# A windowed attention and a SoLU layer on one core: the last 64 rows of a^T on array halves, a late row scale, and sums of three by the reduce

## The chip, the core and the metric

The kernel runs on one core of one Trainium2 chip. Five engines work side by side, each through its own queue in order: PE (matrix products; its weight loads are shown as PEld), DVE (vector operations), ACT (activation functions with a scale and a bias), POOL (elementwise operations) and SP (which here only issues transfers). The metric is the device time of one execution in microseconds.

## The reference

Input x has 8 batches of 4160 rows of 192 numbers; each row has, for each of 8 heads, 7 weights over itself and the 6 rows before it.

```python
w = weight_gen - np.max(weight_gen, axis=-1, keepdims=True)
w = np.exp(w)
w = w / (np.sum(w, axis=-1, keepdims=True) + 1e-09)
...
out = np.einsum('bshk,bskhg->bshg', w, x_unf)        # 7 taps, 8 heads of 24
...
h = x @ w_in                                         # 192 -> 1024
e = np.exp(h - np.max(h, axis=-1, keepdims=True))
sm = e / (np.sum(e, axis=-1, keepdims=True) + 1e-09)
solu = h * sm
mu = np.mean(solu, axis=-1, keepdims=True)
var = np.mean((solu - mu) ** 2, axis=-1, keepdims=True)
ln = (solu - mu) / np.sqrt(var + 1e-06) * g_ln
return (ln @ w_out).astype(np.float32)               # 1024 -> 192
```

The result has 33280 rows of 192. The 1024-wide weights come as 64-bit floats and are turned into 32-bit ones on the chip.

## The kernel before

**Tiles and stages.** Each of 128 partitions takes 260 consecutive rows; tile t is row t of all partitions, so there are 260 tiles of 128 rows. x and the tap weights are loaded in chunks of mostly 16 tiles. The softmax of a chunk's taps (lines 102 to 128) is spread over DVE, POOL and ACT. The attention then works on groups of four tiles (at the start two of two): POOL multiplies seven shifted rows with their weights (L133, output `pr`), adds three of the products to three others (L139), and adds again with two sums out (`half`, L141); DVE's `last_sum` adds these two (L379) into `a`.

For a tile, PE turns `a` (L396) so that its 192 columns lie on partitions. The last 64 of them have first been copied (`copy_columns`) beside themselves, so that the second turned block holds rows 128 to 191 twice, on partitions 0-63 and 64-127. ACT rounds the result to the reduced 32-bit type `x_hi` (L404); the remainder `x_lo` is made by PE and ACT (L411, L418) for three of four tiles by pairs, or by DVE (L426, L427) for every second pair. The first product (`first_product`, L440) takes ten matmuls of 512 columns, five for each half of the 1024 outputs: three for the first 128 rows (high x high, high x low, low x high) and two for the last 64, where the stationary block holds the high part on 64 partitions and the low part on the other 64, and the moving weights `wb_hi`, `wb_lo` are the same 64 rows twice.

The product `h` stays in PSUM, in three buffers of two banks each. Then, tile by tile: DVE's row maximum (L454), a bound of the row (`bound`, L458) and its reciprocal (`row_scale`, L463); ACT's exponentials (L467); DVE's product of h, the row scale and e in place (`solu`, L473); ACT's squares (L479); ACT's 16-bit high half (L486) and DVE's 16-bit low half (L490); a transposing transfer (L498); 24 matmuls of the second product (L542); and ACT's scaled output (L553). The row factors of the output are worked out for four tiles at once in `scales`, in eight short steps on ACT and DVE (L510 to L529).

**Order.** Every engine's queue is written out before the program runs. `issue_order` holds a list of steps with an engine, a cost and the steps they wait for, plays them through, and takes at each moment the ready step of lowest tile number plus a number from the table `URGENCY`. Its names: attA and attB are the POOL operations, fin the last sum, mm1 and mm2 the products, vb and vr bound and reciprocal, hi and lo the halves, f0 to f7 the steps of `scales`, b0 to b5 the conversion of the last 64 rows of `w_in`, and p3 to p8 the preparation of the second weights, which borrows buffers of h at the start.

Of the kernel before, what the change touches and what calls it, by code (L numbers as in the profile page):

```python
# [26 lines left out]
def tile_kernel(ctx: ExitStack, tc: tile.TileContext, x, weight_gen, w_in, w_out, g_ln, out):  # L27
# [102 lines left out]
    def attention(xt, wt, t, n, half):  # L130
# [8 lines left out]
        nc.gpsimd.tensor_tensor(out=pr[:, :3], in0=pr[:, :3], in1=pr[:, 3:6], op=ALU.add)  # L139

        nc.gpsimd.tensor_tensor(  # L141
            out=half, in0=window(pr, 0, [(2 * TG * D, 2), (D, n), (1, D)]),
            in1=window(pr, TG * D, [(5 * TG * D, 2), (D, n), (1, D)]), op=ALU.add,
# [19 lines left out]

    minus = const.tile([P, 2, P], F32R, name="minus")
    nc.vector.tensor_scalar_mul(minus[:, 0, :], ident, -1.0)
    nc.vector.memset(minus.bitcast(F32)[:, 1, :], 0.0)
    nc.vector.tensor_scalar_mul(minus[D2:, 1, :], ident[D2:, :], -1.0)
    minus = [minus[:, n, :] for n in range(2)]
# [205 lines left out]
    def last_sum(t):  # L374
        if t % TG == 0:

            a_of[t // TG] = att.tile([P, TG, 2 * P], F32, name="a", bufs=3)
# [1 line left out]
        nc.vector.tensor_reduce(  # L379
            columns(t)[:, :, :D], half.rearrange("p j t d -> p t d j"), axis=AX.X, op=ALU.add  # L380
# [34 lines left out]
    def low_x(t):
# [3 lines left out]
        for i in range(2):  # L419
            xt_of[t + i] = (hi[:, 0, i, :], lo[:, 0, i, :], lo[:, 1, i, :])  # L420

    def low_x_on_vector(t):
# [3 lines left out]
        sub(out=lo[:, 0], in0=pa[:, 0], in1=hi[:, 0].bitcast(F32), op=ALU.subtract)  # L426
        sub(  # L427
            out=hi[D2:, 1], in0=pa[D2:, 1], in1=hi[D2:, 1].bitcast(F32), op=ALU.subtract
        )
# [429 lines left out]
```

## Time and profile before

| | |
|---|---|
| median of 3 runs | 1400.43 us (1398.85 to 1400.59) |
| the profiled execution | 1399.32 us, span 1397.5 us |
| granted TensorE clock | 0.987 |
| PE, DVE, POOL, ACT busy | 1252.0, 1249.2, 1247.8, 1130.3 us |
| moved by transfers | 211.43 MB, 151 GB/s |

How to read it: the profile is one execution. A group's line gives source line, engine, operation, output<-inputs with shapes, the count, busy time in us and the mean of one in ns, then the idle time of that engine just before these operations and what ended it. In a row by time the first two numbers are start and duration in us. In the table by stage, the stretch is followed by busy time (and instruction count) of each engine. Ends of matmuls are modelled, so their starts are the safer reading. Idle time of an engine that is not the bound costs nothing.

### The profile page before, as it was taken

The page shows a single profiled execution, that of the slowest core. Times are in us where ns is not written, and L with a number is a line of the kernel's source. Part 1 is how long each engine was busy: PE and PEld are TensorE (multiplying, and loading weights), DVE is VectorE, ACT ScalarE, POOL GpSimd, SP SyncE. Part 2 cuts the span into 40 slices and gives each one's busy share as a digit, 9 for nine tenths or more (in the row PEclk, how much of TensorE's full clock was granted, in tenths as well). Part 3 has the DMA queues.
Part 4 walks back from the last instruction along what each step waited for, and adds up shares of the span by engine and source line. Part 5 has one row for each costly group of instructions (what it writes and reads, how often), then busy time and mean ns, then how long its engine had stood idle before and what let it go on. Part 6 is the DMA issues. An engine that isn't in the chain of part 4 may idle for free.

```text
span 1397.5 us, 25636 instructions
## 1 busy us (share of the span) xinstructions
PE 1252.0 (90%) x9508; PEld 1074.0 (77%) x9508; DVE 1249.2 (89%) x2135; ACT 1130.3 (81%) x2231; POOL 1247.8 (89%) x243
## 2 busy tenths in 40 slices
PE   0398999989999998989999999989999899999997
PEld 0277878878788787878888787878878788888786
DVE  2988999989999998899899999989999999999984
ACT  1577888878888887888788888878887888888885
POOL 1999999999999999999999999999999999998000
PEclk9999999999999999999999999999999999999999
DMA  3567769687878877786959777686969687656665
GB/s 94 168 146 177 152 131 200 135 182 129 184 129 173 168 145 159 132 203 123 199 111 191 142 149 171 131 183 125 209 112 207 117 184 144 129 118 129 128 123 121
DMA packets 565878, 211.43 MB, mean 151 GB/s; under 512 B 544457, under 2 KB 545913, under 8 KB 565752
## 3 DMA queue, kind: packets, MB, share of 16 engines
q1 hardware_dynamic: 565752, 209.78, 72.7%
q8 instruction: 75, 1.23, 0.4%
q14 instruction: 51, 0.42, 0.1%
HBM read 46.19 MB, written 25.56 MB: 51 GB/s over the span
## 4 chain that ended last, share of the span: by engine, by line
POOL 50%; DVE 18%; issue 13%; ACT 13%; PE 3%; DMA 2%; SPq 1%; POOLq 0%; DVEq 0%; ACTq 0%
POOL pr L133 26%; POOL pr L139 14%; POOL half L141 6%; DVE h L473 5%; ACT e L479 4%; ACT hl L486 4%; DVE stats L454 3%; DVE hl L490 3%; DVE a L379 2%; ACT e L467 2%; PE h L440 2%; POOL wt L114 2%; POOL wt L126 2%; DMA raw_a<-in_moe_w_in_dram 1%; PE po L542 1%
## 5 line engine op out<-in xcount | busy, mean ns | idle before, releaser
L133 POOL TENSOR_TENSOR pr<-xt,wt 128x5376 f32<-128x5376 f32 (+1 forms) x66 | 631.6, 9569 | 22.5 <-DMA xt<-zeros 19.8
L542 PE MATMUL po<-w_hl,hlT 128*128 128x192 f16 x6192 | 560.5, 248 | 27.7 <-ACT ot L553 26.8
L542 PEld LDWEIGHTS <-hlT 128*128 128x128 f16 x6240 | 519.0, 98 | 72.8 <-issue 70.0
L473 DVE SCALAR_TENSOR_TENSOR h<-h,stats,e 128x1024 f32<-128x1024 f32 x260 | 335.0, 1288 | 23.0 <-ACT e L467 11.2
L490 DVE SCALAR_TENSOR_TENSOR hl<-h,hl 128x1024 f16<-128x1024 f32 x260 | 316.8, 1220 | 34.0 <-ACT e L479 28.3
L486 ACT ACTIVATE hl<-h 128x1024 f16<-128x1024 f32 x260 | 267.5, 1029 | 96.5 <-DVE stats L510 53.2
L139 POOL TENSOR_TENSOR pr<-pr 128x2304 f32<-128x2304 f32 (+1 forms) x66 | 333.2, 5048 | 5.2
L454 DVE TENSOR_REDUCE stats<-h 128x1 f32<-128x1024 f32 x260 | 316.4, 1217 | 10.1 <-PE h L440 9.6
L467 ACT ACTIVATE e<-h,stats 128x1024 f32<-128x1024 f32 x260 | 292.7, 1126 | 34.2 <-DVE stats L454 30.0
L479 ACT ACTIVATE e<-h,stats 128x1024 f32<-128x1024 f32 x260 | 292.3, 1126 | 15.4 <-DVE hl L490 15.3
L440 PE MATMUL h<-wa_hi,x_hi 128*128 128x512 f32 x520 | 226.0, 435 | 40.2 <-ACT e L479 17.7
L141 POOL TENSOR_TENSOR half<-pr 128x1536 f32<-128x1536 f32 (+1 forms) x66 | 226.1, 3426 | 5.2
L440 PE MATMUL h<-wa_lo,x_hi 128*128 128x512 f32 x520 | 207.1, 398 | 0.0
L440 PE MATMUL h<-wa_hi,x_lo 128*128 128x512 f32 x520 | 206.6, 397 | 0.0
L440 PEld LDWEIGHTS h<-wa_hi,x_hi 128*128 128x128 f32 x520 | 99.3, 191 | 64.2 <-ACT e L479 23.2
L396 PE MATMUL pa<-ident,a 128*128 128x128 f32 x520 | 80.4, 277 | 46.4 <-DVE a L379 44.0
L379 DVE TENSOR_REDUCE a<-half 128x768 f32<-128x1536 f32 (+1 forms) x66 | 116.6, 1766 | 1.2 <-POOL half L141 1.2
L440 PEld LDWEIGHTS h<-wa_hi,x_lo 128*128 128x128 f32 x520 | 99.1, 191 | 23.3 <-ACT x_lo L418 0.2
L553 ACT ACTIVATE ot<-po,stats 128x192 f32<-128x192 f32 x258 | 111.0, 430 | 4.9 <-PE po L542 4.8
L396 PEld LDWEIGHTS pa<-ident,a 128*128 128x128 f32 x520 | 64.9, 143 | 62.3 <-DVE a L379 44.0
L440 PEld LDWEIGHTS h<-wa_lo,x_hi 128*128 128x128 f32 x520 | 99.8, 192 | 12.3
L440 PE MATMUL h<-wb_lo,x_lo 128*128 128x512 f32 x260 | 103.7, 399 | 0.0
(84 smaller groups left out, 1308.4 us busy)
## 6 DMA issues: line engine op xcount, KB each, us to landing
out_dram<-ot SPq DMA_DIRECT2D x65, 384.0 KB, 3.2
xt<-in_x_dram SPq DMA_DIRECT2D x30, 576.0 KB, 4.8
xt<-in_x_dram SPq DMA_DIRECT2D x30, 480.0 KB, 4.3
wt<-in_weight_gen_dram SPq DMA_DIRECT2D x15, 448.0 KB, 4.8
hlT<-hl SPq DMA_TRANSPOSE x260, 4.5
raw<-in_moe_w_out_dram SPq DMA_DIRECT2D x1, 1536.0 KB, 9.3
xt<-in_x_dram SPq DMA_DIRECT2D x3, 384.0 KB, 5.6
raw_a<-in_moe_w_in_dram SPq DMA_DIRECT2D x2, 512.0 KB, 11.4
```

The lines of the kernel that those rows point to most:

```text
L133: nc.gpsimd.tensor_tensor(out=window(pr, 0, [(TG * D, K), (HG, n * H), (1, HG)]), in0=window(xt, t * D, [(D, K), (HG, n * H), (1, HG)]), i ...
L139: nc.gpsimd.tensor_tensor(out=pr[:, :3], in0=pr[:, :3], in1=pr[:, 3:6], op=ALU.add)
L141: nc.gpsimd.tensor_tensor(out=half, in0=window(pr, 0, [(2 * TG * D, 2), (D, n), (1, D)]), in1=window(pr, TG * D, [(5 * TG * D, 2), (D, n), ...
L396: nc.tensor.matmul(pa[:, n, i, :], a[:, (t + i) % TG, n * P : (n + 1) * P], ident, is_transpose=True, start=i == n == 0, stop=i == n == 1,)
L440: nc.tensor.matmul(h[:, fs], lhs, rhs[:, fs], start=n == 0, stop=n == len(terms) - 1)
L454: nc.vector.tensor_reduce(stat(t, NMAX), h_of[t], axis=AX.X, op=ALU.max, negate=True)
L467: nc.scalar.activation(e, h_of[t], AF.Exp, bias=stat(t, NMAX), accum_out=stat(t, Z))
L473: nc.vector.scalar_tensor_tensor(out=h, in0=h, scalar=stat(t, SIGMA), in1=e, op0=ALU.mult, op1=ALU.mult, accum_out=stat(t, M))
L479: nc.scalar.activation(e_of.pop(t), h_of[t], AF.Square, bias=stat(t, M), scale=-float(FF), accum_out=stat(t, Q),)
L486: nc.scalar.activation(hl[:, 0, :], h_of[t], AF.Copy, scale=2.0**14)
L490: nc.vector.scalar_tensor_tensor(out=hl[:, 1, :], in0=h_of[t], scalar=2.0**14, in1=hl[:, 0, :], op0=ALU.mult, op1=ALU.subtract,)
L542: nc.tensor.matmul(po[:, :D], hlT[:, half * NJ + j, :], w2_hl[:, j, w, :], start=n == 0, stop=n == len(terms) - 1,)
```

## The change

- *Last 64 rows.* `wb_hi` and `wb_lo` hold output columns 0-511 on partitions 0-63 and columns 512-1023 on partitions 64-127, just as they were converted; the eight transfers of step b5 are gone. The first product takes the first 128 rows in six matmuls, then six matmuls on 64 rows each: for each of three terms one on partitions 0-63 for the first half of the outputs and one on partitions 64-127 for the second. `x_lo` is now the remainder on both halves, by one DVE operation of 512 columns for the pairs that DVE makes.
- *Row scale.* Bound and reciprocal are made for two tiles at once, after the odd one's maximum. `solu` multiplies by a constant; the row scale is read by the high half and the low half instead. `scales` has six steps, and the output factor takes the bound in.
- *Sums of three.* POOL's first add goes to a tile `third` of three sums, its second adds the seventh product to the first of them (768 elements a group, before 1536); the last sum on DVE adds three.
- *Order.* Steps, costs and waits follow, and `URGENCY` has other numbers throughout.

```diff
@@ -44,6 +44,9 @@
     D2 = D - P
     FH = FF // 2
 
+    S_UNIT = 2.0**14
+    UNIT = S_UNIT * FF**1.5
+
...
@@ -136,11 +139,9 @@
             in1=window(wt, t * HK, [(1, K), (K, n * H), (0, HG)]),
             op=ALU.mult,
         )
-        nc.gpsimd.tensor_tensor(out=pr[:, :3], in0=pr[:, :3], in1=pr[:, 3:6], op=ALU.add)
-
+        nc.gpsimd.tensor_tensor(out=third, in0=pr[:, :3], in1=pr[:, 3:6], op=ALU.add)
         nc.gpsimd.tensor_tensor(
-            out=half, in0=window(pr, 0, [(2 * TG * D, 2), (D, n), (1, D)]),
-            in1=window(pr, TG * D, [(5 * TG * D, 2), (D, n), (1, D)]), op=ALU.add,
+            out=third[:, 0], in0=third[:, 0], in1=pr[:, 6], op=ALU.add
         )
     load_w(0)
...
@@ -222,27 +221,18 @@
     first = {}
     wa_hi = const.tile([P, FF], F32R, name="wa_hi")
     wa_lo = const.tile([P, FF], F32R, name="wa_lo")
-    wb_hi = const.tile([P, FF], F32R, name="wb_hi")
-    wb_lo = const.tile([P, FF], F32R, name="wb_lo")
+    wb_hi = const.tile([P, FH], F32R, name="wb_hi")
+    wb_lo = const.tile([P, FH], F32R, name="wb_lo")
     def last_rows(step):
-        if step == 0:
-            first["hl"] = big.tile([P, 2, FH], F32, name="raw_b", bufs=1)
-        hi, lo = (first["hl"][:, n, :].bitcast(F32R) for n in range(2))
         if step < 3:
             first["b"] = float_of_double("b", raw_b, FH, step)
         elif step == 3:
-            nc.scalar.copy(hi, first["b"])
+            nc.scalar.copy(wb_hi, first["b"])
         elif step == 4:
-            nc.vector.tensor_tensor(out=lo, in0=first["b"], in1=hi.bitcast(F32), op=ALU.subtract)
-        elif step == 5:
-            for src, dst in ((hi, wb_hi), (lo, wb_lo)):
-                for n in range(2):
-                    for f in range(2):
-                        nc.sync.dma_start(
-                            dst.bitcast(F32)[n * D2 : (n + 1) * D2, f * FH : (f + 1) * FH],
-                            src.bitcast(F32)[f * D2 : (f + 1) * D2, :],
-                        )
+            nc.vector.tensor_tensor(
+                out=wb_lo, in0=first["b"], in1=wb_hi.bitcast(F32), op=ALU.subtract
+            )
     def first_rows(f, step):
         fs = slice(f * FH, (f + 1) * FH)
...
@@ -375,9 +365,9 @@
         if t % TG == 0:
             a_of[t // TG] = att.tile([P, TG, 2 * P], F32, name="a", bufs=3)
-        half = half_of.pop(t)
+        third = third_of.pop(t)
         nc.vector.tensor_reduce(
-            columns(t)[:, :, :D], half.rearrange("p j t d -> p t d j"), axis=AX.X, op=ALU.add
+            columns(t)[:, :, :D], third.rearrange("p j t d -> p t d j"), axis=AX.X, op=ALU.add
         )
     def copy_columns(t):
...
@@ -409,7 +399,7 @@
         pa, hi = x_parts[t]
         for n in range(2):
             nc.tensor.matmul(
-                pa[:, n], minus[n], hi[:, n], start=False, stop=n == 1, skip_group_check=True
+                pa[:, n], minus, hi[:, n], start=False, stop=n == 1, skip_group_check=True
             )
     def low_x(t):
...
@@ -417,34 +407,34 @@
         lo = small.tile([P, 2, 2, P], F32R, name="x_lo", bufs=2)
         nc.scalar.copy(lo, pa)
         for i in range(2):
-            xt_of[t + i] = (hi[:, 0, i, :], lo[:, 0, i, :], lo[:, 1, i, :])
+            xt_of[t + i] = hi[:, :, i, :], lo[:, :, i, :]
     def low_x_on_vector(t):
         pa, hi = x_parts.pop(t)
         lo = small.tile([P, 2, 2, P], F32R, name="x_lo", bufs=2)
-        sub = nc.vector.tensor_tensor
-        sub(out=lo[:, 0], in0=pa[:, 0], in1=hi[:, 0].bitcast(F32), op=ALU.subtract)
-        sub(
-            out=hi[D2:, 1], in0=pa[D2:, 1], in1=hi[D2:, 1].bitcast(F32), op=ALU.subtract
-        )
+        nc.vector.tensor_tensor(out=lo, in0=pa, in1=hi.bitcast(F32), op=ALU.subtract)
         for i in range(2):
-            xt_of[t + i] = (hi[:, 0, i, :], lo[:, 0, i, :], hi[:, 1, i, :])
+            xt_of[t + i] = hi[:, :, i, :], lo[:, :, i, :]
     def first_product(t):
-        xa, xl, xb = xt_of.pop(t)
+        hi, lo = xt_of.pop(t)
         h = ps_h.tile([P, FF], F32, name="h")
-        terms = [(xa, wa_hi), (xa, wa_lo), (xl, wa_hi), (xb, wb_hi), (xb, wb_lo)]
-        for f in range(2):
-            fs = slice(f * FH, (f + 1) * FH)
-            for n, (lhs, rhs) in enumerate(terms):
+        halves = [slice(f * FH, (f + 1) * FH) for f in range(2)]
+        for fs in halves:
+            for n, (lhs, rhs) in enumerate(((hi, wa_hi), (hi, wa_lo), (lo, wa_hi))):
+                nc.tensor.matmul(h[:, fs], lhs[:, 0, :], rhs[:, fs], start=n == 0, stop=False)
+
+        for n, (lhs, rhs) in enumerate(((hi, wb_hi), (hi, wb_lo), (lo, wb_hi))):
+            for f, fs in enumerate(halves):
+                rows = slice(f * D2, (f + 1) * D2)
                 nc.tensor.matmul(
-                    h[:, fs], lhs, rhs[:, fs], start=n == 0, stop=n == len(terms) - 1
+                    h[:, fs], lhs[rows, 1, :], rhs[rows], start=False, stop=n == 2,
                 )
         h_of[t] = h
 
-    ZE, SIGMA, Q, E, Y, V, Y2, R, OUT, M, Z, U, L, T, NMAX, HALF, BOUND = range(17)
-    stats = const.tile([P, 6, TG, 17], F32, name="stats")
+    Q, E, Y, V, Y2, R, BOUND, OUT, M, Z, L, T, NMAX, HALF, SIGMA = range(15)
+    stats = const.tile([P, 6, TG, 15], F32, name="stats")
     nc.gpsimd.memset(stats[:, :, :, HALF], 0.5)
     def stat(t, which, n=1):
...
@@ -455,12 +445,15 @@
 
     def bound(t):
+        rows = stats[:, t // TG % 6, t % TG - 1 : t % TG + 1, :]
         nc.vector.tensor_reduce(
-            stat(t, BOUND), stat(t, NMAX, 2), axis=AX.X, op=ALU.max, apply_absolute_value=True
+            rows[:, :, BOUND], rows[:, :, NMAX : HALF + 1], axis=AX.X, op=ALU.max,
+            apply_absolute_value=True,
         )
     def row_scale(t):
-        nc.vector.reciprocal(stat(t, SIGMA), stat(t, BOUND))
+        rows = stats[:, t // TG % 6, t % TG - 1 : t % TG + 1, :]
+        nc.vector.reciprocal(rows[:, :, SIGMA], rows[:, :, BOUND])
...
@@ -471,7 +464,7 @@
     def solu(t):
         h, e = h_of[t], e_of[t]
         nc.vector.scalar_tensor_tensor(
-            out=h, in0=h, scalar=stat(t, SIGMA), in1=e, op0=ALU.mult, op1=ALU.mult, accum_out=stat(t, M)
+            out=h, in0=h, scalar=S_UNIT, in1=e, op0=ALU.mult, op1=ALU.mult, accum_out=stat(t, M)
         )
...
@@ -483,12 +476,12 @@
     def high_half(t):
         hl = hl_of[t] = big.tile([P, 2, FF], F16, name="hl", bufs=3)
-        nc.scalar.activation(hl[:, 0, :], h_of[t], AF.Copy, scale=2.0**14)
+        nc.scalar.activation(hl[:, 0, :], h_of[t], AF.Copy, scale=stat(t, SIGMA))
     def low_half(t):
         hl = hl_of[t]
         nc.vector.scalar_tensor_tensor(
-            out=hl[:, 1, :], in0=h_of[t], scalar=2.0**14, in1=hl[:, 0, :],
+            out=hl[:, 1, :], in0=h_of[t], scalar=stat(t, SIGMA), in1=hl[:, 0, :],
             op0=ALU.mult, op1=ALU.subtract,
         )
 
@@ -510,27 +503,23 @@
             nc.vector.tensor_reduce(rows[:, :, out], of(first, n), axis=AX.X, op=op)
         if step == 0:
-            nc.scalar.activation(of(ZE), of(Z), AF.Copy, bias=1e-9)
+            nc.scalar.activation(of(E), of(Z), AF.Square, bias=tiny, scale=1e-3 * UNIT)
         elif step == 1:
-            reduce(U, ZE, 2, ALU.mult)
+            reduce(V, Q, 2, ALU.add)
         elif step == 2:
-            nc.scalar.activation(of(E), of(U), AF.Square, scale=1e-3 * FF**1.5)
-        elif step == 3:
-            reduce(V, Q, 2, ALU.add)
-        elif step == 4:
-            nc.scalar.activation(of(L), of(V), AF.Ln)
+            nc.scalar.activation(of(L), of(V), AF.Ln, scale=UNIT**-2)
             nc.scalar.activation(
                 rows[:, :, Y : Y2 + 1 : 2], of(L).broadcast_to([P, n, 2]), AF.Exp, scale=-0.5
             )
-        elif step == 5:
+        elif step == 3:
             reduce(T, Y, 3, ALU.mult)
-        elif step == 6:
+        elif step == 4:
             nc.scalar.activation(
                 of(R), of(T), AF.Identity, bias=newton[:, 1:2], scale=newton[:, :1]
             )
-        elif step == 7:
-            reduce(OUT, Y2, 2, ALU.mult)
+        elif step == 5:
+            reduce(OUT, Y2, 3, ALU.mult)
 
...
@@ -650,9 +639,8 @@
             once(f"q{f}0", ACT, 700, part + "2")
             once(f"q{f}1", PE, 660, f"q{f}0", *([f"q{f - 1}1"] if f else []))
             once(f"q{f}2", ACT, 520, f"q{f}0")
-    once("b5", SP, 0, "b4")
-    for half in "01":
-        once("p3" + half, DVE, 868, "q31", "mm1" if half == "0" else "q30", *(["p30"] if half == "1" else []))
+    add("p30", 0, DVE, 868, ("q31", 0), ("mm1", 1))
+    once("p31", DVE, 868, "p30", "sq", "lo")
...
@@ -700,11 +688,11 @@
             after.append(("t6", starts[c]))
         if c > 1:
             after.append((f"lx{loads - 1}", starts[c]))
-        add("attA", t, POOL, 14206 if full else 7302, *after, ready=21100 if c == 1 else 0)
-        add("attB", t, POOL, 3380 if full else 1764, ("attA", t), ("fin", groups[i - 2] if i > 1 else -1))
+        add("attA", t, POOL, 9700 if full else 4950, *after, ready=21100 if c == 1 else 0)
+        add("attB", t, POOL, 6900 if full else 3500, ("attA", t), ("fin", groups[i - 2] if i > 1 else -1))
         old = t // 4 * 4 - 12
         add("dup", t, ACT, 307 if full else 200, ("fin", t))
-        add("fin", t, DVE, 1660 if full else 860, ("attB", t), ("xT", old + 2 if old >= 0 else -1))
+        add("fin", t, DVE, 2460 if full else 1260, ("attB", t), ("xT", old + 2 if old >= 0 else -1))
 
...
@@ -718,26 +706,27 @@
         add("xT", t, PE, 600, ("dup", group_of[t]), low_of(t - 2))
         add("xhi", t, ACT, 478, ("xT", t), ("mm1", t - 3))
         if on_vector(t):
-            add("xld", t, DVE, 664, ("xhi", t), ("mm1", t - 3))
+            add("xld", t, DVE, 560, ("xhi", t), ("mm1", t - 3))
         else:
             add("xn", t, PE, 250, ("xhi", t))
             add("xlo", t, ACT, 478, ("xn", t), ("mm1", t - 3))
     stats_of = {u: t for t in range(run) for u in range(t - stat_group(t) + 1, t + 1)}
     for t in range(run):
-        after = [("b5", 0), ("a04", 0), ("a14", 0)] if t == 0 else []
+        after = [("b4", 0), ("a04", 0), ("a14", 0)] if t == 0 else []
         if t < 3:
 
-            after += ([("q10", 0), ("c30", 0)], [("p31", 0), ("sq", 0), ("lo", 0)], [("p80", 0)])[t]
-        if t == 3:
-            after.append(("p81", 0))
-        add("mm1", t, PE, 2250, low_of(t), ("sq", t - 3), ("lo", t - 3), *after)
+            after += ([("q10", 0), ("c30", 0)], [("q20", 0)], [("p31", 0), ("sq", 1), ("lo", 1)])[t]
+        elif t < 5:
+            after.append(("p80" if t == 3 else "p81", 0))
+        add("mm1", t, PE, 2300, low_of(t), ("sq", t - 3), ("lo", t - 3), *after)
         add("max", t, DVE, 1131, ("mm1", t), ("exp", t - 4))
-        add("vb", t, DVE, 70, ("max", t), ("f7", stats_of[t - 24] if t >= 24 else -1))
-        add("vr", t, DVE, 70, ("vb", t))
+        if t % 2:
+            add("vb", t, DVE, 70, ("max", t), ("max", t - 1), ("f5", stats_of[t - 24] if t >= 24 else -1))
+            add("vr", t, DVE, 70, ("vb", t))
         add("exp", t, ACT, 1091, ("max", t), ("sq", t - 2))
-        add("solu", t, DVE, 1210, ("exp", t), ("vr", t))
+        add("solu", t, DVE, 1210, ("exp", t))
         add("sq", t, ACT, 1091, ("solu", t))
-        add("hi", t, ACT, 904, ("solu", t), ("tr", t - 3))
+        add("hi", t, ACT, 904, ("solu", t), ("vr", t | 1), ("tr", t - 3))
         add("lo", t, DVE, 1135, ("hi", t))
         add("tr", t, SP, 1792, ("lo", t), ("mm2", t - 6))
         after = [("p80", 0), ("p81", 0)] if t == 0 else []
@@ -745,18 +734,16 @@
             after += [("mm1", run - 1), ("out", t - 2)]
         else:
             after.append(("out", t - 1))
-        add("mm2", t, PE, 2280, ("tr", t), *after)
-        add("out", t, ACT, 304, ("mm2", t), ("f7", stats_of[t]), ("od", t // 4 * 4 - 5))
+        add("mm2", t, PE, 2200, ("tr", t), *after)
+        add("out", t, ACT, 304, ("mm2", t), ("f5", stats_of[t]), ("od", t // 4 * 4 - 5))
         if n := stat_group(t):
             tiles = range(t - n + 1, t + 1)
             add("f0", t, ACT, 200, *(("exp", u) for u in tiles))
-            add("f1", t, DVE, 70, ("f0", t), *(("vr", u) for u in tiles))
-            add("f2", t, ACT, 200, ("f1", t))
-            add("f3", t, DVE, 70, ("f2", t), *(("sq", u) for u in tiles))
-            add("f4", t, ACT, 400, ("f3", t))
-            add("f5", t, DVE, 70, ("f4", t))
-            add("f6", t, ACT, 200, ("f5", t), ("p4", 0))
-            add("f7", t, DVE, 70, ("f6", t))
+            add("f1", t, DVE, 70, ("f0", t), *(("sq", u) for u in tiles))
+            add("f2", t, ACT, 400, ("f1", t))
+            add("f3", t, DVE, 70, ("f2", t))
+            add("f4", t, ACT, 200, ("f3", t), ("p4", 0))
+            add("f5", t, DVE, 70, ("f4", t), *(("vr", u | 1) for u in tiles))
         if t % 4 == 3:
             add("od", t, SP, 1092, ("out", t))
 
...
```

More of the change, by code (lines that the diff above doesn't have):

```diff
@@ L128, in softmax_taps, with attention @@
             )
-    def attention(xt, wt, t, n, half):
+    def attention(xt, wt, t, n, third):
         pr = att.tile([P, K, TG, D], F32, name="pr", bufs=1)[:, :, :n]
@@ L162, in tile_kernel @@
     sq = const.tile([P, 4], F32, name="sq")
[L164 to L168, printed above, removed]
+    tiny = const.tile([P, 1], F32, name="tiny")
+    nc.vector.memset(tiny, 1e-9 * 1e-3 * UNIT)
+    minus = const.tile([P, P], F32R, name="minus")
+    nc.vector.tensor_scalar_mul(minus, ident, -1.0)
     raw_a = att.tile([P, 2 * FF], I32, name="raw_a", bufs=1)
@@ L319, in prepare_second @@
             )
-            nc.vector.tensor_scalar_add(kinv, k, (127 - 73 + 1) << 23)
+            nc.vector.tensor_scalar_add(kinv, k, (127 - 73 - 14) << 23)
             nc.vector.tensor_scalar(k, k, -1, (127 + 73) << 23, op0=ALU.mult, op1=ALU.add)
@@ L324, in prepare_second @@
             nc.scalar.copy(k, second["total"][:, 9:10])
-            for n, factor in enumerate((-0.5, 1.5)):
+            for n, factor in enumerate((-0.5 * UNIT**-2, 1.5)):
                 nc.scalar.activation(
@@ L348, in tile_kernel @@
     p_of = {}
-    half_of = {}
+    third_of = {}
     o_of = {}
@@ L366, in attend @@
         c = max(n for n in range(NCHUNK) if starts[n] <= t)
-        half = att.tile([P, 2, TG, D], F32, name="half", bufs=2)[:, :, :n]
-        half_of[t] = half
-        attention(xs[c], ws[c], t - starts[c], n, half)
+        third = att.tile([P, 3, TG, D], F32, name="third", bufs=2)[:, :, :n]
+        third_of[t] = third
+        attention(xs[c], ws[c], t - starts[c], n, third)
     def columns(t):
@@ L572, in tile_kernel @@
     )
-    for n in range(6):
+    for n in range(5):
         ops[f"b{n}"] = once(last_rows, n)
@@ L588, in tile_kernel @@
         ops[f"lx{n}"] = at_chunk(load_x, n)
-    for n in range(8):
+    for n in range(6):
         ops[f"f{n}"] = at(scales, n)
@@ L601 @@
 URGENCY = dict(
[L602 to L611 removed]
+    a00=25.6, a01=-4.1, a02=0.4, a03=20.4, a04=-2.7, a10=78.5, a11=165.5, a12=5.2, a13=30.2,
+    a14=-71.1, attA=-31.6, attB=-36.1, b0=-61.1, b1=28.5, b2=-2.6, b3=-6.3, b4=147.1, c00=-41.9,
+    c01=19.2, c02=47.5, c10=-7.7, c11=8.7, c12=-60.4, c20=118, c21=1.5, c22=-83.1, c30=117.2,
+    c31=100.9, c32=-135.6, dup=99.1, exp=-62.9, f0=114.1, f1=-43.1, f2=10.2, f3=-95.5, f4=15,
+    f5=1.2, fin=24.3, hi=-114.6, lo=-151.2, lw=-13.6, lx0=47.1, lx1=121.3, lx2=60.1, lx3=-38.1,
+    max=-11.8, mm1=132.4, mm2=81.3, od=37.4, out=14.6, p30=-34.8, p31=-75.6, p4=-1.5, p5=2.2,
+    p6=-81.3, p70=0.8, p71=29.5, p80=129.2, p81=-32.4, q00=7.8, q01=-102.7, q02=63.1, q10=-1.5,
+    q11=-11.5, q12=45.4, q20=-136, q21=19.1, q22=11.4, q30=-112.8, q31=-132.6, q32=89.3, solu=-1.5,
+    sq=117, t0=13.3, t1=-25, t2=91.8, t3=-6.1, t4=-8.9, t5=4.5, t6=-84.2, tr=135, vb=-89.7,
+    vr=-103.4, xT=-140.9, xhi=12.9, xld=-4.6, xlo=-7.1, xn=72.4,
 )
@@ L801, in issue_order @@
                 busy = end
-        if name == "b5":
-            free[e], end = time + 480, time + 5360
-            queue = end - 2000
-        elif e == SP:
+        if e == SP:
             queue = max(queue, time) + (625 if name == "tr" else 450)
```

10 lines of the change are left out of this document (removed).

## The prediction

> **What bounds the kernel now.** I read the page's busy table and its chain of waits first, then the busy time by stage, then one stage row by row.
>
> ```profile
> span 1397.5 us, 25636 instructions
> PE 1252.0 (90%) x9508; PEld 1074.0 (77%) x9508; DVE 1249.2 (89%) x2135; ACT 1130.3 (81%) x2231; POOL 1247.8 (89%) x243
> POOL 50%; DVE 18%; issue 13%; ACT 13%; PE 3%; DMA 2%; SPq 1%; POOLq 0%; DVEq 0%; ACTq 0%
> ```
>
> Three engines stand at 89 to 90%, and the chain names POOL for half the span. That would make the shorter attention sum on POOL the part that pays. The stage table and the line of the last sum (L379) say otherwise:
>
> ```profile
> core 0: us, PE busy (x) PEld busy (x) DVE busy (x) ACT busy (x) POOL busy (x), PEclk, DMA share, GB/s
> 200.00:1130.00 930.00, 875.30 (x6684) 752.16 (x6683) 861.40 (x1461) 783.81 (x1537) 920.67 (x170) 0.99 0.78 158
> 1162.00:1361.00 199.00, 188.76 (x1465) 163.28 (x1464) 179.58 (x309) 166.03 (x328) 125.67 (x21) 1.00 0.64 127
> core 0: us, DVE busy (x), PEclk, DMA share, GB/s
> 200.00:1130.00 930.00, 221.91 (x183) 0.99 0.78 158
> 1162.00:1361.00 199.00, 48.71 (x40) 1.00 0.64 127
> ```
>
> The second pair of rows counts only the row maximum (L454), one per tile: 183 tiles in 930 us is 5.08 us a tile, 40 in 199 us is 4.98. In the first stretch PE is busy 875.30/930 = 94%, DVE 93%, ACT 84%. POOL is at 99%, yet it is ahead of the others:
>
> ```profile
> L379 DVE TENSOR_REDUCE a<-half x66: 959/1790/1829, 42.9 to 1304.7; 128x768 f32<-128x1536 f32 x64, 128x384 f32<-128x768 f32 x2
>   POOL half L141: 1.2, 2
> L133 POOL TENSOR_TENSOR pr<-xt,wt 128x5376 f32<-128x5376 f32 x64 | 621.7, 9714 | 2.7
> L139 POOL TENSOR_TENSOR pr<-pr 128x2304 f32<-128x2304 f32 x64 | 327.9, 5124 | 5.0
> L141 POOL TENSOR_TENSOR half<-pr 128x1536 f32<-128x1536 f32 x64 | 222.5, 3476 | 5.0
> ```
>
> In the whole run DVE waited for POOL's sums 1.2 us. The last of them, of POOL's last output, starts at 1304.7, 93 us before the end. So POOL's time is nearly balanced with the others' until late in the run, but it is not what the tiles wait for: PE, DVE and ACT, handing each tile round in an order written out beforehand, make the 5.08 us. PE is the fullest of them.
>
> **What a microsecond of load is worth.** The two stretches differ in the softmax of the taps, which is over before the second:
>
> ```profile
> L112 DVE TENSOR_REDUCE wm<-wt 128x128 f32<-128x896 f32 (+2 forms) x18 | 17.8, 988 | 2.8 <-DMA wt<-in_weight_gen_dram 2.8
> L120 DVE TENSOR_REDUCE wm<-wt 128x128 f32<-128x896 f32 (+2 forms) x18 | 17.8, 988 | 12.4 <-ACT wt L118 12.4
> L124 DVE RECIPROCAL wy<-wy 128x128 f32<-128x128 f32 (+2 forms) x18 | 15.6, 866 | 0.3 <-ACT wy L122 0.3
> ```
>
> That is 51.2/260 = 0.20 us of DVE a tile, and without it a tile takes 0.10 to 0.11 us less. So about half of a load that one of the coupled engines gains or loses reaches the end. I use one half; the bounds are 0 and 1.
>
> **PE: the array halves.** Before, a tile's first product is ten matmuls of 512 columns. After, it is six of them on 128 rows and six on 64 rows, three pairs in which one works on rows 0-63 and the other on rows 64-127, into different PSUM banks.
>
> ```profile
> 600.41 0.40 PE L440 MATMUL h<-wb_hi,x_hi 128*128 128x512 f32 x1
> 600.64 0.40 PE L440 MATMUL h<-wb_lo,x_hi 128*128 128x512 f32 x1
> 600.88 0.40 PE L440 MATMUL h<-wa_hi,x_hi 128*128 128x512 f32 x1
> ```
>
> Matmuls start 0.23 us apart but each record is 0.40 us long: 0.17 us of a matmul is hidden under the next. No row here has a matmul on 64 rows, so the price has two ends. If a pair runs at once, the product takes nine slots, 9 x 0.23 = 2.07 us for 2.30, a gain of 0.23. If the halves run one after another it takes twelve, 2.76, a loss of 0.46. Besides, the array changes its division twice a tile (into halves, and back for the matmul that follows). If each change must let the running matmul finish, the hidden 0.17 us comes to light twice, 0.34. I take pairs at once and both tails, because nothing in the trace shows such a change hidden: 2.07 + 0.34 = 2.41, **+0.11 us a tile**; ends -0.23 and +0.80.
>
> The Trainium skill bears on both halves of this choice. "TensorEngine Tiling (Array Packing)", section Key Properties, says that a change of tiling mode, not of tile, drains the TensorE; it gives no time, and no run here shows it yet. "TensorE: Matmul & The Clock Gate", section Measured speedup vs the span model, lets a pack last one matmul and about 4 ns more per tile; by that alone the product would take an estimated 2.08 us.
>
> **DVE.** The last sum reads 2304 elements a group of four tiles instead of 1536.
>
> ```profile
> 55.31 0.96 DVE L379 TENSOR_REDUCE a<-half 128x384 f32<-128x768 f32 x1
> 601.87 1.79 DVE L379 TENSOR_REDUCE a<-half 128x768 f32<-128x1536 f32 x1
> L463 DVE RECIPROCAL stats<-stats 128x1 f32<-128x1 f32 x260 | 41.7, 161 | 5.7
> L458 DVE TENSOR_REDUCE stats<-stats 128x1 f32<-128x2 f32 x260 | 38.3, 147 | 2.2
> L510 DVE TENSOR_REDUCE stats<-stats 128x4 f32<-128x8 f32 (+3 forms) x268 | 42.1, 157 | 13.4 <-ACT e L479 7.9 <-ACT stats L529 4.5 <-ACT stats L523 0.7
> L427 DVE TENSOR_TENSOR x_hi<-pa,x_hi 64x256 fp32r<-64x256 f32 x65 | 27.8, 428 | 1.4
> L426 DVE TENSOR_TENSOR x_lo<-pa,x_hi 128x256 fp32r<-128x256 f32 x65 | 27.1, 417 | 5.4 <-ACT x_hi L404 5.1
> L254 DVE TENSOR_TENSOR wa_lo<-h,wa_hi 128x512 fp32r<-128x512 f32 x2 | 1.4, 680 | 0.0
> ```
>
> The step of 768 inputs costs 1.79 - 0.96 = 0.83 us, so +0.83/4 = +0.21 a tile. Bound and reciprocal for two tiles at once drop one of each per two tiles: 0.31/2 = -0.15 by duration; such small operations overlap their neighbours, so I take -0.11. One of four small reductions per group goes (-0.157/4 = -0.04; -0.02 where overlapped; I take -0.03). L426 and L427 become one operation of 512, priced by L254: (0.68 - 0.85)/4 = -0.04. The scale read per row moves from the product with e (L473) to the low half (L490):
>
> ```profile
> L473 DVE SCALAR_TENSOR_TENSOR h<-h,stats,e 128x1024 f32<-128x1024 f32 x260 | 335.0, 1288 | 23.0 <-ACT e L467 11.2
> L490 DVE SCALAR_TENSOR_TENSOR hl<-h,hl 128x1024 f16<-128x1024 f32 x260 | 316.8, 1220 | 34.0 <-ACT e L479 28.3
> L467 ACT ACTIVATE e<-h,stats 128x1024 f32<-128x1024 f32 x260 | 292.7, 1126 | 34.2 <-DVE stats L454 30.0
> L486 ACT ACTIVATE hl<-h 128x1024 f16<-128x1024 f32 x260 | 267.5, 1029 | 96.5 <-DVE stats L510 53.2
> ```
>
> L473's 0.07 us over L490 is either the row scale, which then only moves, or the accumulator, which stays and lets L490 gain 0.07; I take 0. Sum: 0.21 - 0.11 - 0.03 - 0.04 = **+0.03**; ends -0.04 and +0.13.
>
> **ACT.** The high half gets a scale read per row. The nearest row with such an operand is L467, 0.10 us longer than L486: +0.10 a tile, less one small operation per group of four. Net about +0.05. ACT is idle 16% of the long stretch, and I cost it at nothing; without that cover half of it, 0.025 a tile, is 6 us.
>
> **POOL and start.** The second add falls from 1536 to 768 elements, which the two-tile groups show at 1.81 us: 3.48 - 1.81 = 1.67 us a group, 110 us of POOL over the run. It is worth little where POOL is ahead, and the 1.2 us of waiting at most. At the start POOL does lead:
>
> ```profile
> 49.71 1.81 POOL L141 TENSOR_TENSOR half<-pr 128x768 f32<-128x768 f32 x1
> 67.43 3.47 POOL L141 TENSOR_TENSOR half<-pr 128x1536 f32<-128x1536 f32 x1
> ```
>
> By tile 4 two small groups (0.9 us each, of which POOL's wait for the taps takes one back) and one full one have passed: 0.9 + 1.7, about **-3 us**, once. The first product of tile 1 no longer waits for the weights' preparation, and the eight transfers that copied the last rows are gone, but tile 4 comes from POOL in any case; I count nothing for them.
>
> **Sum.** (0.11 + 0.03)/2 = 0.07 us a tile, times the 255 tiles behind the start, is +18; minus 3 is +15. Some of the tails will fall where PE waits anyway (it is idle 6%), which takes off about 3. +12 on the profiled execution's 1399.3 us (1.8 around its span) is **1411 us**; that execution lies within the three shown, 1.1 under their median.
>
> **Rivals.**
> *Free changes of division.* If the tails stay hidden, PE loses 0.23 a tile: (-0.23 + 0.03)/2 x 255 - 3 = -28, **1371 us**. For it: PE is the fullest engine, and it passes from the first product (L440) to the half-precision one (L542) without a gap, the usual 0.23 us later. Against it: those all use 128 rows.
>
> ```profile
> 606.80 0.40 PE L440 MATMUL h<-wb_lo,x_hi 128*128 128x512 f32 x1
> 607.04 0.34 PE L542 MATMUL po<-w_hl,hlT 128*128 128x192 f16 x2
> ```
>
> Its place is the two ends of the three pairs, and it decides once a change costs under about 0.11 us, where -0.23 + 2 x 0.11 + 0.03 is near zero.
> *The halves don't run at once.* Then PE needs 875.30/183 = 4.78 + 0.46 = 5.24 us a tile at least, more than the present pace; at its present 94% that is 5.57, +0.49 x 255 = +125, **1524 us**; without idle time about 1440.
> *The even tile waits for the odd one's bound.* Its high half now needs the maximum of the next tile:
>
> ```profile
> 608.52 1.22 DVE L454 TENSOR_REDUCE stats<-h 128x1 f32<-128x1024 f32 x1
> 608.83 1.05 ACT L486 ACTIVATE hl<-h 128x1024 f16<-128x1024 f32 x1
> ```
>
> That high half belongs to the tile before this maximum; it could start only at about 610.1, 1.3 us later, with the squares, exponentials and output scaling of ACT's queue behind it, low half and transpose after it. Half of 1.3/2 a tile is 0.33 x 255 = +83, about **1490 us** if the order leaves it there always. The order is made anew with this dependency in it, which can move a maximum ahead, so I give it little.
> *Balance.* Tails of about 0.11 and the terms cancel: **1399 us**.
>
> **Chances.** Forecast 0.47, free changes 0.28, not at once 0.08, even tile 0.09, balance 0.08. The forecast's own range is 1396 to 1440 (all of the load passed on: 0.14 x 255 = +36). The range with the free changes is 1366 to 1440; deeper gains (all of 0.20 passed on is -54) and the two late rivals are left out. Under 0.2% nothing can be told from no change. Faster: 0.26 from the free changes, 0.02 of the balance and 0.09 from the forecast's low side, 0.37; the same 0.13; slower 0.50.
>
> **What will show it.** The start-to-start distance of the two matmuls of a pair (near zero, or 0.23) and the gaps before the first and after the last pair (0 or 0.17) settle PE's term. The last sum should take about 2.6 us, the high half 1.13, the POOL add 1.8. If the pace of the long stretch is under 5.0 us a tile, I am wrong about the changes of division; if DVE waits long for POOL at the last sum, about POOL; if ACT's high half waits far more than its 96.5 us, the even tile is the cause.

## The result and the profile after

The changed kernel takes 1412.41 us (median of 4, 1411.94 to 1412.8) against 1399.91 for the one before in the same comparison: 1.009 times as long, 95% interval 1.0072 to 1.0107. The forecast was 1411. The total came out as forecast; the places in which the time was lost did not, as the rows below show.

The page of the kernel after, its busy table and chain of waits:

```profile
span 1410.2 us, 26003 instructions
PE 1258.7 (89%) x10028; PEld 988.3 (70%) x10028; DVE 1260.5 (89%) x1742; ACT 1149.5 (82%) x2164; POOL 1140.1 (81%) x243
DVE 44%; ACT 14%; issue 14%; POOL 13%; PE 11%; DMA 3%; SPq 1%; ACTq 0%; DVEq 0%; POOLq 0%
```

POOL lost 1247.8 - 1140.1 = 108 us and fell from 50% to 13% of the chain, yet the end came later. DVE's busy time rose by 11.3 us, and DVE now leads the chain.

The same kernel's groups by line (busy us, mean ns, idle before and its releaser):

```profile
L369 DVE TENSOR_REDUCE a<-third 128x768 f32<-128x2304 f32 (+1 forms) x66 | 182.4, 2763 | 0.0
L466 DVE SCALAR_TENSOR_TENSOR h<-h,e 128x1024 f32<-128x1024 f32 x260 | 318.4, 1225 | 54.9 <-ACT e L460 53.6
L483 DVE SCALAR_TENSOR_TENSOR hl<-h,stats,hl 128x1024 f16<-128x1024 f32 x260 | 329.2, 1279 | 13.7 <-ACT e L472 10.1 <-ACT hl L479 2.7
L456 DVE RECIPROCAL stats<-stats 128x2 f32<-128x2 f32 x130 | 21.6, 166 | 1.7
L449 DVE TENSOR_REDUCE stats<-stats 128x2 f32<-128x4 f32 x130 | 20.1, 155 | 1.0
L415 DVE TENSOR_TENSOR x_lo<-pa,x_hi 128x512 fp32r<-128x512 f32 x65 | 44.4, 684 | 14.5 <-ACT x_hi L394 14.5
L479 ACT ACTIVATE hl<-h,stats 128x1024 f16<-128x1024 f32 x260 | 285.8, 1120 | 7.6 <-DVE stats L456 3.8 <-DVE h L466 3.0
L142 POOL TENSOR_TENSOR third<-pr 128x2304 f32<-128x2304 f32 (+1 forms) x66 | 332.7, 5041 | 82.3 <-DVE a L369 53.9 <-DVE stats L449 21.4 <-DVE stats L456 3.5
```

The last sum is 1.0 us longer; it never waits for POOL. POOL stands idle 82.3 us before its first add, the first writer of the partial sums; 53.9 of it ends when DVE has taken earlier ones. The row scale moved 0.06 us from one DVE operation to the other, as the forecast had it. ACT's high half, which by the rival of the even tile should have waited more, waits 7.6 us where it waited 96.5. The waiting has moved ahead in ACT's queue: the exponentials (L460) now wait 64.9 us for 34.2, the squares (L472) 30.9 for 15.4.

The PE rows of one tile in time order (start, duration in us; "x2" is a pair):

```profile
602.88 0.47 PE L425 MATMUL h<-wa_hi,x_hi 128*128 128x512 f32 x1
603.20 0.39 PE L425 MATMUL h<-wa_lo,x_hi 128*128 128x512 f32 x1
603.43 0.39 PE L425 MATMUL h<-wa_hi,x_lo 128*128 128x512 f32 x1
...
604.11 0.40 PE L425 MATMUL h<-wa_hi,x_lo 128*128 128x512 f32 x1
604.44 0.50 PE L430 MATMUL h<-wb_hi,x_hi 64*128 64x512 f32 x2
604.78 0.40 PE L430 MATMUL h<-wb_lo,x_hi 64*128 64x512 f32 x2
605.01 0.40 PE L430 MATMUL h<-wb_hi,x_lo 64*128 64x512 f32 x2
605.34 0.34 PE L531 MATMUL po<-w_hl,hlT 128*128 128x192 f16 x2
```

The two matmuls of a pair run together: they share a row, and the next pair starts 0.23 us after the second one, the time of a single matmul. Against these 0.23 us, the step into the halves takes 0.33, the first pair 0.34, the step out 0.33: 0.31 us for both changes of division, in three places. The product is 5 x 0.23 + 0.33 + 0.34 + 0.23 + 0.33 = 2.38 us, where 2.41 was forecast and 2.30 stood before.

Where the time went, by the count of row maxima (one per tile) in three stretches; the fourth row has the last sums in the first stretch. A row gives the stretch, its length, DVE's busy time on these operations and their count. First the kernel before, then the changed one:

```profile
0.00:270.00 270.00, 49.74 (x41) 0.97 0.67 151
270.00:1162.00 892.00, 213.07 (x175) 0.99 0.78 158
1162.00:1370.00 208.00, 51.14 (x42) 1.00 0.64 126
0.00:270.00 270.00, 19.89 (x12) 0.97 0.67 151
```

```profile
0.00:270.00 270.00, 46.04 (x38) 0.97 0.61 140
270.00:1162.00 892.00, 212.23 (x175) 0.99 0.77 158
1162.00:1370.00 208.00, 52.09 (x43) 1.00 0.69 130
0.00:270.00 270.00, 33.81 (x13) 0.97 0.61 140
```

By 270 us the changed kernel is three tiles behind. In the long stretch both do 175 tiles; at the end the changed one gains one back. The starts of the 41st, the 216th and the last row maximum say it more finely, first before, then changed:

```profile
268.41 1.22 DVE L454 TENSOR_REDUCE stats<-h 128x1 f32<-128x1024 f32 x1
1157.84 1.23 DVE L454 TENSOR_REDUCE stats<-h 128x1 f32<-128x1024 f32 x1 [0.40 <-PE h L440]
1376.25 1.22 DVE L454 TENSOR_REDUCE stats<-h 128x1 f32<-128x1024 f32 x1
```

```profile
280.75 1.21 DVE L444 TENSOR_REDUCE stats<-h 128x1 f32<-128x1024 f32 x1
1177.07 1.23 DVE L444 TENSOR_REDUCE stats<-h 128x1 f32<-128x1024 f32 x1
1389.15 1.22 DVE L444 TENSOR_REDUCE stats<-h 128x1 f32<-128x1024 f32 x1 [0.17 <-PE h L430]
```

The changed kernel is 12.3 us late at the 41st tile, 19.2 at the 216th and 12.9 at the last: what it loses, it has lost by 270 us. In that stretch DVE spent 33.81 us on 13 last sums, 19.89 on 12 before, 14 us more; the experiments show how little of the loss this is.

### The profile page after: what moved, and what is told of

Same layout as the page of the kernel before. It is cut to its first block, busy times and chain, and to the rows that moved or that the text cites. A ratio compares the mean times of both kernels' runs of the same rounds, so it can differ in the third digit from the quotient of the medians.

```text
span 1410.2 us, 26003 instructions
## 1 busy us (share of the span) xinstructions
PE 1258.7 (89%) x10028; PEld 988.3 (70%) x10028; DVE 1260.5 (89%) x1742; ACT 1149.5 (82%) x2164; POOL 1140.1 (81%) x243
## 4 chain that ended last, share of the span: by engine, by line
DVE 44%; ACT 14%; issue 14%; POOL 13%; PE 11%; DMA 3%; SPq 1%; ACTq 0%; DVEq 0%; POOLq 0%
DVE hl L483 12%; DVE stats L444 10%; DVE a L369 10%; DVE h L466 7%; POOL pr L136 6%; ACT e L472 5%; PE h L425 4%; PE po L531 4%; POOL third L142 4%; ACT e L460 3%; ACT hl L479 3%; PE h L430 2%; POOL third L143 1%; DMA raw_a<-in_moe_w_in_dram 1%; DVE x_lo L415 1%
## 5 line engine op out<-in xcount | busy, mean ns | idle before, releaser
L142 POOL TENSOR_TENSOR third<-pr 128x2304 f32<-128x2304 f32 (+1 forms) x66 | 332.7, 5041 | 82.3 <-DVE a L369 53.9
L466 DVE SCALAR_TENSOR_TENSOR h<-h,e 128x1024 f32<-128x1024 f32 x260 | 318.4, 1225 | 54.9 <-ACT e L460 53.6
L460 ACT ACTIVATE e<-h,stats 128x1024 f32<-128x1024 f32 x260 | 292.5, 1125 | 64.9 <-DVE stats L444 63.5
L483 DVE SCALAR_TENSOR_TENSOR hl<-h,stats,hl 128x1024 f16<-128x1024 f32 x260 | 329.2, 1279 | 13.7 <-ACT e L472 10.1
L472 ACT ACTIVATE e<-h,stats 128x1024 f32<-128x1024 f32 x260 | 291.1, 1121 | 30.9 <-DVE h L466 14.1
L479 ACT ACTIVATE hl<-h,stats 128x1024 f16<-128x1024 f32 x260 | 285.8, 1120 | 7.6 <-DVE stats L456 3.8
L369 DVE TENSOR_REDUCE a<-third 128x768 f32<-128x2304 f32 (+1 forms) x66 | 182.4, 2763 | 0.0
L386 PE MATMUL pa<-ident,a 128*128 128x128 f32 x520 | 86.8, 290 | 66.5 <-DVE a L369 42.8
L386 PEld LDWEIGHTS pa<-ident,a 128*128 128x128 f32 x520 | 56.0, 143 | 112.3 <-DVE a L369 42.2
L430 PE MATMUL h<-wb_hi,x_hi 64*128 64x512 f32 x520 | 131.2, 501 | 0.0
L143 POOL TENSOR_TENSOR third<-third,pr 128x768 f32<-128x768 f32 (+1 forms) x66 | 118.5, 1795 | 5.2
L430 PEld LDWEIGHTS h<-wb_hi,x_hi 64*128 64x128 f32 x520 | 48.6, 184 | 94.2 <-issue 94.2
```

The costliest lines, as they stand in the source:

```text
L142: nc.gpsimd.tensor_tensor(out=third, in0=pr[:, :3], in1=pr[:, 3:6], op=ALU.add)
L369: nc.vector.tensor_reduce(columns(t)[:, :, :D], third.rearrange("p j t d -> p t d j"), axis=AX.X, op=ALU.add)
L430: nc.tensor.matmul(h[:, fs], lhs[rows, 1, :], rhs[rows], start=False, stop=n == 2,)
L460: nc.scalar.activation(e, h_of[t], AF.Exp, bias=stat(t, NMAX), accum_out=stat(t, Z))
L466: nc.vector.scalar_tensor_tensor(out=h, in0=h, scalar=S_UNIT, in1=e, op0=ALU.mult, op1=ALU.mult, accum_out=stat(t, M))
L472: nc.scalar.activation(e_of.pop(t), h_of[t], AF.Square, bias=stat(t, M), scale=-float(FF), accum_out=stat(t, Q),)
```

## The experiments

Medians of four executions, each beside the kernel before on the same chip (1399.1 to 1399.8 us there).

### One part alone

**Array halves alone,** every queue in the order of before:

```diff
-        terms = [(xa, wa_hi), (xa, wa_lo), (xl, wa_hi), (xb, wb_hi), (xb, wb_lo)]
...
+        for n, (lhs, rhs) in enumerate(((hi, wb_hi), (hi, wb_lo), (lo, wb_hi))):
+            for f, fs in enumerate(halves):
+                rows = slice(f * D2, (f + 1) * D2)
...
```

> The kernel before with the array halves alone; every queue in the order of before (the step of the eight copies stays in the plan and does nothing). Theory of loads (half of what a coupled engine gains or loses reaches the end): the product takes 2.38 us for 2.30 (pairs at once, the changes of division cost 0.31), DVE saves 0.04 a tile: (0.07 - 0.04)/2 x 255 = +4, 1404 us. Rival, the changes of division carry the whole loss: 1412 us. Rival, the halves gain and the loss is elsewhere: under 1397 us.

1394.13 us, ratio 0.996 (0.9945 to 0.9974). A gain of 5.6 us where the theory had a loss of 4: DVE is busy 1229.7 us, 19.5 less, and PE 0.08 us a tile more. The last rival held: the halves don't carry the loss.

**Sums of three alone,** same order:

```diff
-            out=half, in0=window(pr, 0, [(2 * TG * D, 2), (D, n), (1, D)]),
...
+            out=third[:, 0], in0=third[:, 0], in1=pr[:, 6], op=ALU.add
...
```

> The kernel before with the sums of three alone, every queue in the order of before. The last sum took 2.80 us after for 1.79 before, +0.25 us of DVE a tile. Theory of loads: half of it, 0.125 x 255 = +32, 1432 us. If DVE alone sets the pace: all of it, +64, 1464 us. Rival, POOL sets the pace (its chain share is 50% before) and DVE has room: 1.67 us less per group of POOL, under 1395 us.

1441.19 us, ratio 1.0291 (1.0274 to 1.0308): +41 us for 65.6 us more on DVE, 63% of it passed on. A POOL 105 us lighter gave nothing that shows beside it. This bears out, for this order, that POOL was not what the tiles wait for.

**Late row scale alone,** with the old urgencies:

```diff
-            out=h, in0=h, scalar=stat(t, SIGMA), in1=e, op0=ALU.mult, op1=ALU.mult, accum_out=stat(t, M)
+            out=h, in0=h, scalar=S_UNIT, in1=e, op0=ALU.mult, op1=ALU.mult, accum_out=stat(t, M)
...
-        add("hi", t, ACT, 904, ("solu", t), ("tr", t - 3))
+        add("hi", t, ACT, 904, ("solu", t), ("vr", t | 1), ("tr", t - 3))
```

> The kernel before with the late row scale for two tiles alone; steps, waits and the order of the start follow, as they must (with the old start the plan has a circle: tile 0 waits for tile 1's maximum, tile 1's product for tile 0's buffer). Theory of loads: DVE saves about 0.13 us a tile, ACT gains 0.07, order of the start costs 7 to 12 us: -0.065 x 255 + 10 = -7, about 1393 us. Rival, the even tile's wait for the odd one's bound carries the loss: 1412 us or more.

1451.09 us, ratio 1.036 (1.0341 to 1.038), with less work on DVE (1229.4 us busy). The theory of loads missed by 58 us. Its order could not be held, so either the wait or the order made with the old urgencies was to blame. ACT's high half (L494) waited only 9.4 us here, so a short wait there doesn't clear the even tile.

**The other table of urgencies alone** (same work as before):

> The kernel before with the other kernel's table of urgencies (the steps it lacks get the value of a neighbour). Same work, another order. Theory of loads: 1400 us within 5. Rival, the order carries the loss: 1410 us or more, with the first products of tiles 4 to 40 some 7 to 12 us later as in the changed kernel.

1420.7 us, ratio 1.0149 (1.0134 to 1.0164). The order alone is worth more than the whole change. Its row maxima in the first stretch:

```profile
0.00:270.00 270.00, 46.29 (x38) 0.96 0.64 144
```

38 tiles, as in the changed kernel: this table of urgencies loses the start by itself, on the old work. The 41st row maximum starts at 281.04 us, 12.6 late.

### One part undone

**Sums of three undone,** in the changed kernel's order:

> The changed kernel with the sums of three undone (halves and late scale stay), every queue in the order of the changed kernel. Alone on the kernel before the sums of three cost 41 us. Theory of loads: half to two thirds of 0.25 us of DVE a tile comes back, 32 to 41 us, 1371 to 1380 us, faster than both kernels. Rival, POOL, with 1.67 us more a group, becomes what this order waits for: 1395 us or more.

1439.79 us, 27 us slower than the changed kernel: the rival held. DVE now waits for POOL at the last sum, and ACT waits longer for POOL's part of the taps' softmax, with DVE behind it. The waits of this run (total us, times, longest), then those of the changed kernel:

```profile
DVE a L371 <- POOL half L144: 14.5, 6, 6.2
ACT wt L121 <- POOL wt L117: 81.0, 12, 12.9
DVE wm L123 <- ACT wt L121: 39.0, 6, 10.1
```

```profile
ACT wt L121 <- POOL wt L117: 34.8, 7, 8.4
DVE wm L123 <- ACT wt L121: 9.8, 5, 3.0
```

The order had been planned for the shorter POOL. So POOL's 1.67 us a group, of which nothing showed in the order of before, is needed in this one.

**Array halves undone,** in the changed kernel's order:

> The changed kernel with the array halves undone (ten matmuls on 128 rows, two DVE operations for the remainder), every queue in its order. Theory of loads, with the 6 us that the halves gained alone: about 1418 us. Rival, the changes of division are the price of the changed kernel: under 1408 us.

1431.23 us, 19 us slower than the changed kernel and 13 above the theory. DVE is busy 1280.6 us, 20 more. The halves are a gain here too, and a larger one than the 6 us that they gained alone.

### One engine's load

**One pair of matmuls fewer:**

```diff
-        for n, (lhs, rhs) in enumerate(((hi, wb_hi), (hi, wb_lo), (lo, wb_hi))):
+        for n, (lhs, rhs) in enumerate(((hi, wb_hi), (hi, wb_lo))):
...
```

> The changed kernel without the third pair of matmuls (low part of the last 64 rows times the high weights is left out, so that part of h's last digits is missing); order unchanged. PE loses 0.23 us a tile. Theory of loads: half of it, -29 us, 1383 us. Rival, DVE sets the pace in the changed kernel: 1405 to 1412 us.

1411.39 us. PE's busy time fell by 49 us and the end by 1.0, inside the noise. PE does not set the pace of the changed kernel.

**One partial sum fewer on DVE:**

```diff
-            columns(t)[:, :, :D], third.rearrange("p j t d -> p t d j"), axis=AX.X, op=ALU.add
+            columns(t)[:, :, :D], third[:, :2].rearrange("p j t d -> p t d j"), axis=AX.X, op=ALU.add
```

> The changed kernel whose last sum reads only two of the three partial sums (two of the seven taps are left out of the result); POOL and every queue's order unchanged. DVE loses about 1.0 us a group, 0.25 us a tile. Where 0.23 us a tile less of PE gave 1 us, theory: DVE sets the pace of the changed kernel, and half to all of this comes back, 1380 to 1348 us. Rival, neither PE nor DVE alone sets it (the order and the waits do): 1400 us or more.

1383.09 us, ratio to the kernel before 0.9882 (0.9868 to 0.9897): 29 us less than the changed kernel for 65.6 us less on DVE (last sum 116.8 us in all), 45%, a little under the theory's half. DVE's load counts in the changed kernel where PE's did not. The chain then passes to PE:

```profile
PE 59%; POOL 14%; DVE 12%; ACT 7%; issue 5%; DMA 2%; SPq 1%; POOLq 0%; DVEq 0%; ACTq 0%
```

The start hardly gains. In the first 270 us its last sums took 21.64 us, 12 less than in the changed kernel, and its 41st row maximum is still 9.5 us late:

```profile
277.87 1.21 DVE L444 TENSOR_REDUCE stats<-h 128x1 f32<-128x1024 f32 x1
```

This run also prices POOL. The kernel with the sums of three undone, in the same order, has the same load on DVE (1203.2 us busy, 1202.3 here) and differs in POOL's adds (1247.0 us busy, 1140.3 here): 1439.79 - 1383.09 = 57 us for 107 us more on POOL.

**Six changes of division instead of two:** the pairs stand between the matmuls on 128 rows.

> The changed kernel with the three pairs set between the matmuls on 128 rows, two of these before each pair: six changes of division a tile instead of two, the same twelve matmuls. A change measured 0.10 to 0.20 us (into the halves 0.20, out of them 0.10): +0.60 us of PE a tile, 5.4 us of PE a tile, above the pace of 5.12. Theory: PE then sets the pace, 1412 + 0.60 x 255 x (0.5 to 1) = 1490 to 1565 us. Rival, the changes hide under other work when short: under 1430 us.

1559.35 us, ratio 1.1143 (1.1125 to 1.1161). PE rows of one tile:

```profile
600.51 0.71 PE L428 MATMUL h<-wa_hi,x_hi 128*128 128x512 f32 x2
601.15 0.50 PE L432 MATMUL h<-wb_hi,x_hi 64*128 64x512 f32 x2
601.59 0.74 PE L428 MATMUL h<-wa_lo,x_hi 128*128 128x512 f32 x2
602.25 0.50 PE L432 MATMUL h<-wb_lo,x_hi 64*128 64x512 f32 x2
602.69 0.73 PE L428 MATMUL h<-wa_hi,x_lo 128*128 128x512 f32 x2
603.35 0.51 PE L432 MATMUL h<-wb_hi,x_lo 64*128 64x512 f32 x2
603.79 2.15 PE L533 MATMUL po<-w_hl,hlT 128*128 128x192 f16 x24
```

A pair and two whole matmuls take 602.25 - 601.15 = 1.10 us, 3 x 0.23 = 0.69 without a change: 0.41 us for each way in and out, more than the 0.31 above. The whole product takes 603.79 - 600.51 = 3.28 us, against 605.34 - 602.88 = 2.46 in the changed kernel: 0.82 us a tile, 209 us over 255 tiles, and PE's busy time rose by 1467.5 - 1258.7 = 209. Of this 147 us reached the end. PE is then busy 94% of the span and holds 88% of the chain. That the changes cost time, and do not hide, is shown.

### With the order made for the kernel

In three more kernels the table of urgencies was searched anew for the kernel's own steps, with step costs set near the measured durations. No such search was made for the unchanged work, so part of each gain may be the search's.

**Late row scale alone:**

> The kernel before with the late row scale alone, as in the run with the unfitted order (1451 us), but with the table of urgencies searched anew for its own steps and costs. Theory, the loss of 51 us was the order's: 1385 to 1405 us. Rival, the even tile's wait for the odd one's bound costs by itself, whatever the order: 1425 us or more.

1384.46 us, ratio 0.9894 (0.9879 to 0.9909); the same work took 1451 in the other order. The 51 us were the order's, and the even tile's wait can be covered by one. That the wait costs nothing is not shown.

**Array halves alone:**

> The kernel before with the array halves alone and the table of urgencies searched anew for its steps and costs. In the order of before it took 1394 us. Theory, a fitted order is worth some microseconds more: 1382 to 1394 us, faster than both kernels. Rival, the old order was already as good for it: 1394 to 1400 us.

1369.51 us, ratio 0.9784 (0.9768 to 0.9801): 30 us faster than the kernel before, 43 faster than the changed one, and better than forecast. Its chain and its last sum's wait:

```profile
POOL 75%; issue 7%; DVE 5%; PE 5%; ACT 4%; DMA 3%; SPq 0%; POOLq 0%; DVEq 0%; ACTq 0%
L367 DVE TENSOR_REDUCE a<-half 128x768 f32<-128x1536 f32 (+1 forms) x66 | 116.9, 1772 | 22.3 <-POOL half L141 22.2
```

Here DVE does wait for POOL, 22 us, and POOL has 75% of the chain.

**Halves and late scale together:**

> Array halves and late row scale without the sums of three, with the table of urgencies searched anew (in the order of the changed kernel, planned for a shorter POOL, it took 1440 us and DVE waited 14.6 us for POOL's sums). Theory, that loss was the order's, and the late scale's 0.13 us of DVE a tile is worth something on top of the halves: 1375 to 1394 us. Rival, the late scale costs by itself: 1405 us or more.

1393.57 us, ratio 0.9961 (0.9946 to 0.9976), against 1439.79 in the changed kernel's order. It lies at the upper edge of the theory's range: the order was the larger part of that loss. But the theory's other half failed: on top of the halves the late scale did not gain, it lost 24 us against the halves alone (1369.51). Whether a better order exists for it is open, since each search is only as good as its end.

## Why the prediction was right or wrong

**The total was right by luck: two wrong terms made up for one another.** The forecast put +18 us on the long run of tiles, -3 for tails that fall where PE waits anyway, and -3 on the start. Measured: 12.3 us lost by the 41st tile and next to nothing in all the rest (19.2 us late at the 216th, 12.9 at the last).

**PE's price was right, its worth was not.** "Pairs at once and both tails" gave +0.11 us a tile; the rows give +0.08. The forecast's two tails of 0.17 us turned out as three parts of about 0.1: the way in, the first pair, the way out. The sentence of the Trainium skill ("TensorEngine Tiling (Array Packing)", section Key Properties) is that a change of tiling mode drains the TensorE. The trace agrees as far as both ways cost time, 0.33 us for a step of 0.23; since the ends of matmuls are modelled, it can't show whether the array runs quite empty. The step that failed is "about half of a load that one of the coupled engines gains or loses reaches the end", taken from DVE's taps and applied to PE because PE was the fullest. Even for DVE it was not clean: the same softmax of the taps also loads POOL (L114 and L126 of the kernel before, 58.1 us) and ACT (L118 and L122, 21.3 us), and all of it is over before the second stretch that the forecast compared. In the changed kernel 49 us of PE's busy time were worth 1 us. For DVE the same ratio held well: 63% with the sums alone, 45% with a sum taken away. In the sum, PE should have stood near 0 instead of +14. PE's load counted only where there was enough of it to make PE the limit: with six changes of division 147 of 209 us reached the end.

**DVE.** +0.03 us a tile was forecast, 11.3/260 = +0.04 found. Inside it, the last sum was under-priced (+0.25 for +0.21: three inputs an output cost 2.80 us where the step of two gave 2.62), and the small operations about made up for it. Bound and reciprocal fell by 38.3 us, the 0.15 a tile that the forecast had by duration. After overlap, the last sum's 65.8 us, less 10.5 for `x_lo` and 4.2 for the two operations with the row scale, leave 51.1, of which 11.3 show in DVE's busy time: the small operations took off 39.8 us, 0.15 a tile, for 0.11 + 0.03. That the row scale only moves held (0.06 us down on one operation and up on the other).

**ACT and POOL.** The high half's +0.10 was +0.09. ACT's busy time rose by 19.2 us; what this is worth at the end was not measured. POOL's 108 us were not taken away by themselves in the order of before; with the heavier sum on DVE nothing of them showed. And "worth little where POOL is ahead" is a statement about one order: in the order of the changed kernel, 107 us more on POOL cost 57 us with DVE's load held. Undoing the sums of three there gave back about 29 us of DVE's and cost these 57, hence the 27 us of loss.

**The start** is the term that was wrong in sign: -3 forecast, 12.3 found by the 41st tile. The forecast followed POOL's lead up to tile 4 and took DVE's side and the order for free. The table of urgencies alone, on the old work, also does 38 tiles by 270 us and is 12.6 us late at the 41st. With 12 us of the last sum's time taken off DVE in that stretch, the changed kernel was still 9.5 us late there. So most of the loss is not the sums' load, and the order is the likely cause; which of its steps it is was not followed.

**The rivals.** Free changes of division: refuted by the rows, and in this order would not have paid either (a pair of matmuls fewer gave 1 us). Halves one after another: refuted. The even tile's wait: not the +83 us of the rival, since with an order of its own the late scale took 1384 us. The sign named for it, a long wait of the high half, could not tell: that wait was 7.6 us in the changed kernel and 9.4 us in the run of 1451. A smaller cost stays open, as the halves lost 24 us with the late scale on top, each with its own order. What none of the rivals named is the order: the three parts alone came to -6, +41 and +51 us, together to +12.5, and one other table of urgencies moved the same work by 21.

## What to carry to other kernels

Where every queue is written out beforehand, a part can't be judged by its load alone: hold the order, or make it anew for each variant, before you say what a part is worth. The fullest engine need not be the one that pays; take some of its work away and look at the end. A low wait on an engine (DVE's 1.2 us for POOL) tells of the present order only, and the best kernel here, the array halves with an order of their own at 1369.5 us, came to wait for just that engine; how much of its 30 us an order made anew for the unchanged work would have given was not tried.
